# One gated pair of linear attention blocks: kv and M in head blocks of 120, 120 and 80 features a half, and M read back in two loads

## Chip, cores, metric

One core of a Trainium2 chip. The metric is the device time of one execution in microseconds, the median of the runs; lower is better. All times below are in microseconds unless ns is written.

The engines by the names of the profile: PE is TensorE (PEld its weight loads), DVE VectorE, ACT ScalarE, POOL GpSimd, SP SyncE. SP and ACT both issue DMAs, each on a queue of its own.

## The reference

Two linear attention blocks, A and B, read the same `x` (2048 rows, 640 features, 32 heads of 20), each with its own weights; a gate of each row mixes their outputs.

```python
def _A_ref(x, wqkv, wo):          # B is the same with its own weights
    B, S, D = x.shape
    H = 32; Dh = D // H
    qkv = (x @ wqkv).reshape(B, S, 3, H, Dh).transpose(2, 0, 3, 1, 4)
    q, k, v = qkv[0], qkv[1], qkv[2]
    phi = lambda t: jnp.where(t > 0, t + 1, jnp.exp(t)) + 1e-6
    pq, pk = phi(q), phi(k)
    kv = jnp.einsum("bhsd,bhse->bhde", pk, v)
    z = jnp.einsum("bhsd->bhd", pk)
    num = jnp.einsum("bhqd,bhde->bhqe", pq, kv)
    den = jnp.einsum("bhqd,bhd->bhq", pq, z)[..., None] + 1e-6
    return (num / den).transpose(0, 2, 1, 3).reshape(B, S, D) @ wo

g = sigmoid((x * gate_w).sum(-1, keepdims=True))
out = g * a + (1 - g) * b
```

## The kernel before

**What is computed instead of the reference's steps.** The kernel never forms `v`. It builds G = transpose(x) times phi(k), 640 by 640 (the two tiles `GT`, the left and the right 320 columns, the "halves"), and from it kv = transpose(wv) times G, of which only the 20 by 20 blocks of the heads on the diagonal are wanted. kv and the output weights give one 640 by 640 matrix M = kv wo for each branch. The output is then phi(q) of A, scaled by the gate and the denominators, times M of A, plus the same of B. Both large products and most of the others are done with fewer multiplications by sums and differences of quarters (the functions named `strassen`, the products `p1` to `p7` of a `Pair`).

**Order.** Everything from line 955 on is issued in the order in which it is written (`manual_schedule`). Each engine, and each DMA queue, works its own instructions in that order. The program goes: keys and queries of A (to some 50), G of A (50 to 71), keys and queries of B, with the kv of A as one fill between two of its products (72 to 114), M of A and G of B (114 to 139), kv and M of B (137 to 143), and from 141 on the output products, in eight `Pair`s of row blocks.

**kv.** `kv_mm` (L630) makes the diagonal blocks in strips. The 640 output features are cut into six blocks, `f_rows` (L99): five of 120 features, which are six heads, and a last one of 40. `e_rows` (L98) are the 120 weight columns of each, the last one taken from 520 to 640. The block from 240 to 360 lies across the two halves of G, so `pieces` (L100) has seven entries, with two for this block. Each piece is five matmuls, one for each 128 rows of the contraction: the weights of v are the stationary operand (128 rows, 120 columns), and 120, 80 or 40 columns of G are the moving one. The results stand in two PSUM banks, blocks 0 to 3 in the first. `kv_mask` (L641) multiplies them on DVE with `maskE` (L106, built on POOL at L186 to L191), which keeps the head blocks, and writes bf16 into `kv6`.

**M.** `m_block` (L652) multiplies one masked block with its 120 rows of wo: two matmuls of 320 columns. `wo_sb` (`load_wo`, L883) has wo laid out by these blocks; it comes in two DMAs. `m_a` (L667) and `m_b` (L675) copy the result out of PSUM and `m_store` (L664) writes the block's rows to a scratch in HBM, `m_rows`. From there M is read back with five consecutive rows in each partition, which is the layout that the output products need: A's in one load (L552), B's with `m_load` (L683).

**A's kv and M.** The class `Masks` (L1028) is the second fill of the first `q_strassen` of B: its matmuls are issued there, then its masks in two steps (`clamp`, `top`) between other DVE work. It also issues the load of wv of B, in four DMAs. Next in TensorE's order after kvA is the product of L417 that goes on in the bank `co`, which DVE reads at L435 just before. A's M blocks follow at L1062 to L1064 and L551.

**B's kv and M.** `kv_low` (L1068) is called by `g_strassen` (L599) between the two last products of G: the first three pieces, which need only the left half of G. Behind them stand M blocks 0 and 1 (L1075), then the PSUM pool is exchanged for the pool `outer` with six banks, z0, z1, x0, x1, w0, w1 (L1082), which stand where slots 0, 1 and 3 of the old pool were. Then come the other four pieces with their masks, M blocks 2 to 5 among the first output product (`pairs[4].p1`), and three loads of M: blocks 0 and 1 issued by ACT, 2 and 3 and then 4 and 5 by SP. While M comes back, TensorE works on the products that don't need M of B: `p1` of all eight pairs and `p5` of four. The first that needs it is `pairs[0].p2`. `m_b` copies each half block out of PSUM, the first half on ACT, the second on ACT for blocks 0 and 1 and on DVE for the others.

Of the kernel before, what the change touches and what calls it, by code (L numbers as in the profile page):

```python
# [9 lines left out]
P = 128  # L10
FP32 = mybir.dt.float32
BF16 = mybir.dt.bfloat16
ACT = mybir.ActivationFunctionType
ALU = mybir.AluOpType

S, D, H = 2048, 640, 32
Dh = D // H
DT = D // P
# [4 lines left out]
HF = D // 2  # L23
TW = 4
NG = 6
K6 = 120
# [7 lines left out]
def kernel(  # L34
# [11 lines left out]
    nc = tc.nc  # L46
# [4 lines left out]
    persist = ctx.enter_context(tc.tile_pool(name="persist", bufs=1))  # L51
    wpool = ctx.enter_context(tc.tile_pool(name="wpool", bufs=1))
# [34 lines left out]
    def ps(name, slot=None):  # L87

        return banks(ps_raw(name, slot))
# [5 lines left out]
    GT = [persist.tile([P, DT, HF], BF16, name=f"GT{n}") for n in range(2)]  # L95
    M = [persist.tile([P, DT, D], BF16, name=f"M{b}") for b in "AB"]
    wo_sb = [None, None]
    e_rows = [slice(k, k + K6) for k in list(range(0, DT * K6, K6)) + [D - K6]]  # L98
    f_rows = [slice(k, min(k + K6, D)) for k in range(0, D, K6)]  # L99
    pieces = [(g, lo, hi) for g, f in enumerate(f_rows) for lo, hi in (  # L100
        (f.start, min(f.stop, HF)), (max(f.start, HF), f.stop)) if lo < hi]
    ident = persist.tile([P, P], BF16, name="ident")
    I4 = persist.tile([P, H], BF16, name="I4")
    zE = persist.tile([P, 2 * D], BF16, name="zE")
    E4 = zE[:, D:2 * D]
    maskE = persist.tile([P, K6], BF16, name="maskE")  # L106
    spread = persist.tile([P, P], BF16, name="spread")
    R = persist.tile([P, 2, 4, RB], BF16, name="R")
    kv6 = [R[:].rearrange("p h j n -> p (h j n)"), zE[:]]
# [32 lines left out]
    wo_dram = [A_wo, B_wo]  # L142
# [41 lines left out]
        out=spread[:].rearrange("p (h t) -> p h t", t=TW), in_=I4[:, :, None].to_broadcast([P, H, TW])  # L184
    )
    nc.gpsimd.memset(maskE[:], 1.0)  # L186
    for sign, base in ((1, 0), (-1, Dh - 1)):
        nc.gpsimd.affine_select(
            out=maskE[:], in_=maskE[:], pattern=[[-sign * Dh, K6 // Dh], [0, Dh]],
            compare_op=ALU.is_ge, fill=0.0, base=base, channel_multiplier=sign,  # L190
        )  # L191
    nc.gpsimd.memset(E4, 1.0)
    for r in range(4):
        rows = slice(32 * r, 32 * r + 32)
# [432 lines left out]
        nc.vector.tensor_copy(out=zsel[:], in_=pt[:, 0, HF:HF + DT * H].rearrange("p (c h) -> p c h", h=H))  # L627
        return zsel

    def kv_mm(b, banks, pieces, cs=range(DT)):  # L630

        for g, f0, f1 in pieces:
            hf = f0 // HF
            at = f0 - (g - g % 4) * K6
            for k, c in enumerate(cs):
                nc.tensor.matmul(
                    banks[g // 4][:K6, at:at + f1 - f0], lhsT=wv[b][:, c, e_rows[g]],
                    rhs=GT[hf][:, c, f0 - hf * HF:f1 - hf * HF], start=(k == 0), stop=(k == DT - 1),
                )

    def kv_mask(b, banks, g0, g1):  # L641

        n = f_rows[g0].stop - f_rows[g0].start
        count, lo = g1 - g0, f_rows[g0].start
        at = lo - (g0 - g0 % 4) * K6
        nc.vector.tensor_tensor(
            out=kv6[b][:K6, lo:lo + count * n].rearrange("p (g n) -> p g n", g=count),
            in0=banks[g0 // 4][:K6, at:at + count * n].rearrange("p (g n) -> p g n", g=count),
            in1=maskE[:K6, None, K6 - n:K6].to_broadcast([K6, count, n]), op=ALU.mult,
        )  # L650

    def m_block(b, g, banks, to=None):  # L652

        at = f_rows[g].start
        for hf in range(2):
            nc.tensor.matmul(
                banks[hf][:K6, 0:HF], lhsT=kv6[b][:K6, at:at + K6], rhs=wo_sb[b][:K6, g, hf * HF:(hf + 1) * HF],
                start=True, stop=True,
            )
        if to is None:  # L660
            to = work.tile([P, D], BF16, tag="osb", name="m5", bufs=3)
        return to[:f_rows[g].stop - at]

    def m_store(g, to):  # L664
        nc.sync.dma_start(out=m_rows[f_rows[g], :], in_=to)

    def m_a(g, slot):  # L667

# [6 lines left out]
    def m_b(g, banks):  # L675

        to = m_block(1, g, banks, held["mb"][:, g, :] if g < DT else None)
        n = to.shape[0]
        for hf, copy in enumerate((nc.scalar.copy, nc.scalar.copy if g < 2 else nc.vector.tensor_copy)):
            copy(out=to[:, hf * HF:(hf + 1) * HF], in_=banks[hf][:n, 0:HF])  # L680
        m_store(g, to)

    def m_load(g0, g1, eng):  # L683

        rows = slice(f_rows[g0].start, f_rows[g1 - 1].stop)
        eng.dma_start(
            out=M[1][rows.start // DT:rows.stop // DT], in_=m_rows[rows, :].rearrange("(p m) d -> p m d", m=DT)
        )

    def cells(pt):  # L690
        return [pt[:, hf] for hf in range(2)]
# [184 lines left out]
    def load_w(b, which, eng, cuts=(0, DT)):  # L876
        lo = {"q": 0, "k": D, "v": 2 * D}[which]
        t = wpool.tile([P, DT, D], BF16, tag="w" + which, name=f"w{which}{'AB'[b]}")
        for c0, c1 in zip(cuts, cuts[1:]):
            eng.dma_start(out=t[:, c0:c1], in_=wq_dram[b][:, c0:c1, lo:lo + D])  # L880
        return t

    def load_wo(b, eng):  # L883
        wo_sb[b] = wpool.tile([P, NG, D], BF16, tag="wo", name=f"wo{'AB'[b]}")
        eng.dma_start(out=wo_sb[b][:K6, 0:DT], in_=wo_dram[b][0:DT * K6].rearrange("(j p) f -> p j f", p=K6))
        eng.dma_start(out=wo_sb[b][:K6, DT], in_=wo_dram[b][e_rows[DT], :])

    class Nothing:

# [65 lines left out]
    with tc.manual_schedule():  # L955
# [72 lines left out]
        class Masks:  # L1028

            def __init__(self, slot):  # L1030
                self.pt = ps("kvA", slot)
                kv_mm(0, cells(self.pt), pieces)
                wv[1] = load_w(1, "v", nc.sync, (0, 1, 2, 3, DT))

            def clamp(self):
                kv_mask(0, cells(self.pt), 0, 4)

            def top(self):
                kv_mask(0, cells(self.pt), 4, 5)
                kv_mask(0, cells(self.pt), 5, 6)  # L1040

        f = fifth(0, quad[1:3])
# [23 lines left out]
        held["mb"] = wpool.tile([P, DT, D], BF16, tag="wk", name="MBr")  # L1066

        def kv_low():  # L1068
            held["kv"] = cells(ps("kvB", 2))
            kv_mm(1, held["kv"], pieces[:3])  # L1070
            kv_mask(1, held["kv"], 0, 2)

        g_strassen(1, 1, 0, 3, kv_low)
        kv = held["kv"]
        for g, slot in enumerate((3, 0)):  # L1075
            m_b(g, cells(ps("mB", slot)))
        new_stage(None)
        outer = ctx.enter_context(late_pool("outer"))
        t = wpool.tile([P, 2, DT, HF], BF16, tag="wq", name="TM12")
# [1 line left out]
        half = ST // 2  # L1081
        acc = {k: [bank(outer, f"o{k}{n}") for n in range(2)] for k in "zxw"}  # L1082
        pairs = [Pair(i) for i in range(half)]
        kv[1] = acc["x"][1]
        kv_mm(1, kv, pieces[3:5], (2, 3, 4, 0, 1))
        kv_mask(1, kv, 2, 4)
        kv_mm(1, kv, pieces[5:], (2, 3, 4, 0, 1))
        for g in (4, 5):
            kv_mask(1, kv, g, g + 1)
        spare = cells(ps("mB", 2))  # L1090
        pairs[4].p1(None, (0, 1))
        m_b(2, acc["w"])
        m_b(3, spare)
        pairs[4].p1(None, (2, 3, 4))
        m_b(4, acc["z"])
        m_b(5, acc["w"])
        m_load(0, 2, nc.scalar)
        pairs[4].p1_out()
        for g in (2, 4):
            m_load(g, g + 2, nc.sync)  # L1100
        scale(1, 4)
        for rows, ks in ((0, (1,)), (1, (1,)), (0, (2, 4))):
            p_sums(part[rows], ks)
        for k, to in ((5, None), (6, spare[0]), (7, acc["z"][0]), (2, acc["w"][0]), (3, acc["w"][1])):
            pairs[k].p1(to)
        held["p5"] = wpool.tile([P, 2, HF], FP32, tag="wv", name="p5s")
        pairs[0].p1()
# [73 lines left out]
```

## Time and profile before

| | us |
|---|---|
| median of 3 runs (185.88 to 185.99) | 185.98 |
| the profiled execution | 185.64 |
| its span, first to last instruction | 183.90 |
| DVE busy | 149.0 (81%) |
| ACT busy | 108.4 (59%) |
| POOL busy, all of it in the first 10.5 | 9.1 (5%) |
| kv of B on TensorE, 25 + 10 matmuls | 137.6 to 141.3 |
| stores of M of B, first and last issue | 140.74, 144.03 |
| loads of M of B: ACT, SP, SP issue | 143.53, 145.27, 148.28 |

The granted clock of TensorE is 1.0 throughout. The span is what the instructions of the profile cover; the rest of the execution's time lies around it. A line of a timeline or of the chain begins with its start in the span and its length. A line of a group gives what is written from what, shape, count, then busy time and the mean duration in ns of one, then the engine's idle time before them. Matmuls are pipelined, so that the durations of neighbours overlap; what one costs TensorE is the time from its start to the next one's.

### The profile page before, as it was taken

What the parts mean: (1) busy time and instruction counts of PE and PEld (TensorE: products, weight loads), DVE (VectorE), ACT (ScalarE), POOL (GpSimd) and SP (SyncE); (2) the same over time, 40 slices, a digit from 0 to 9 for tenths busy, and PEclk for the clock granted to TensorE, in tenths of its full rate; (3) what the DMA queues carried; (4) which work ended last, traced back from release to release, by engine and by line L of the source; (5) the groups of instructions that cost most, each with busy time, mean ns of one, the idle gap of its engine ahead of it and who ended that gap; (6) DMA issues with size and microseconds to landing.
All of it is one profiled execution on the core that took longest, in us unless ns stands there. A gap on an engine that the chain in (4) does not pass through costs nothing.

```text
span 183.9 us, 3530 instructions
## 1 busy us (share of the span) xinstructions
PE 179.7 (98%) x1357; PEld 121.0 (66%) x1357; DVE 149.0 (81%) x263; ACT 108.4 (59%) x207; POOL 9.1 (5%) x25
## 2 busy tenths in 40 slices
PE   8999999999999999999999999999999999999993
PEld 3656657665667667676666655777678767777772
DVE  0488988999899799798898987969795978778854
ACT  2155589976883553776778787873814637453210
POOL 8920000000000000000000000000000000000000
PEclk9999999999999999999999999999999999999999
DMA  6995449985018000004100000144901820322232
GB/s 182 323 141 86 100 100 302 344 166 179 0 40 249 11 4 0 0 0 133 50 0 0 4 0 2 35 133 144 239 13 42 232 84 4 123 91 77 71 126 88
DMA packets 20896, 18.01 MB, mean 98 GB/s; under 512 B 9168, under 2 KB 20624, under 8 KB 20880
## 3 DMA queue, kind: packets, MB, share of 16 engines
q1 hardware_dynamic: 19952, 16.67, 33.0%
q10 hardware_dynamic: 928, 1.13, 1.9%
q8 instruction: 10, 0.16, 0.4%
q14 instruction: 6, 0.05, 0.1%
HBM read 11.54 MB, written 4.28 MB: 86 GB/s over the span
## 4 chain that ended last, share of the span: by engine, by line
PE 91%; DMA 4%; DVE 2%; ACT 1%; issue 0%; SPq 0%; DVEq 0%
PE gs L519 17%; PE kB L299 12%; PE q L417 11%; PE kA L299 11%; PE qA L352 7%; PE oy L774 6%; PE oz L774 4%; PE ox L774 3%; PE ow L774 3%; PE q L352 3%; PE gA L489 2%; PE gB L489 2%; DMA m_rows<-m 2%; PE warm L211 2%; DMA MB<-m_rows 1%; PE qB L352 1%
## 5 line engine op out<-in xcount | busy, mean ns | idle before, releaser
L299 PEld LDWEIGHTS <-xT 128*128 128x128 bf16 x320 | 30.9, 98 | 14.9 <-DVE xT L257 0.2
L276 DVE TENSOR_SCALAR e<-e 128x640 bf16<-128x640 bf16 (+2 forms) x58 | 20.0, 346 | 6.0 <-ACT e L268 5.6
L299 PE MATMUL kB<-wkB,xT 128*128 128x320 bf16 x160 | 24.2, 299 | 0.0
L299 PE MATMUL kA<-wkA,xT 128*128 128x320 bf16 (+1 forms) x160 | 23.2, 299 | 0.0
L268 ACT ACTIVATE e<-q 128x512 bf16<-128x512 f32 x26 | 15.7, 603 | 5.3 <-PE q L417 4.3
L268 ACT ACTIVATE e<-kB 128x640 bf16<-128x640 f32 x16 | 11.4, 710 | 7.6 <-PE kB L299 7.5
L519 PEld LDWEIGHTS <-xn 128*128 128x128 bf16 x128 | 12.3, 98 | 5.4 <-issue 0.6
L268 ACT ACTIVATE e<-kA 128x640 bf16<-128x640 f32 x16 | 11.3, 713 | 7.4 <-PE kA L299 7.3
L352 PE MATMUL qA<-xT,wqA 128*128 128x512 bf16 x60 | 13.4, 379 | 0.1
L352 PEld LDWEIGHTS <-wqA 128*128 128x128 bf16 x64 | 7.5, 117 | 6.1 <-issue 0.3
L837 ACT COPY u<-ox 128x320 f32<-128x320 f32 x8 | 3.4, 426 | 12.4 <-PE ox L774 12.4
L287 DVE SCALAR_TENSOR_TENSOR pk<-kB,e 128x640 bf16<-128x640 f32 x12 | 9.9, 823 | 1.0
L774 PEld LDWEIGHTS <-pqTB 128*128 128x128 bf16 x80 | 7.7, 98 | 3.7 <-issue 0.7
L774 PEld LDWEIGHTS <-xT 128*128 128x128 bf16 x85 | 8.1, 98 | 2.9
L774 PEld LDWEIGHTS <-pqTA 128*128 128x128 bf16 x85 | 8.0, 98 | 2.9
L779 DVE TENSOR_TENSOR osb<-oz,u 128x320 bf16<-128x320 f32 (+1 forms) x18 | 8.0, 453 | 2.3 <-PE oz L774 1.8
L519 PE MATMUL gs<-pk,xn 128*128 128x320 bf16 x64 | 9.4, 299 | 0.0
L287 DVE SCALAR_TENSOR_TENSOR pk<-kA,e 128x640 bf16<-128x640 f32 x10 | 8.2, 822 | 0.9 <-DVE e L276 0.2
L435 DVE TENSOR_TENSOR q<-q,p 128x512 f32<-128x512 f32 x12 | 8.3, 693 | 0.8 <-PE q L417 0.6
L268 ACT ACTIVATE e<-qA 128x1024 bf16<-128x1024 f32 x6 | 6.2, 1028 | 4.4 <-PE qA L352 4.2
L489 PEld LDWEIGHTS <-xn 128*128 128x128 bf16 x64 | 6.2, 98 | 3.2 <-issue 0.3
L519 PEld LDWEIGHTS <-S 128*128 128x128 bf16 x64 | 6.0, 98 | 2.6 <-issue 0.5
(193 smaller groups left out, 358.5 us busy)
## 6 DMA issues: line engine op xcount, KB each, us to landing
out_dram<-osb SPq DMA_DIRECT2D x14, 160.0 KB, 1.8
xn<-in_A_x_dram SPq DMA_DIRECT2D x3, 640.0 KB, 6.3
wvA<-in_A_wqkv_dram SPq DMA_DIRECT2D x1, 800.0 KB, 10.1
wkB<-in_B_wqkv_dram SPq DMA_DIRECT2D x1, 800.0 KB
wqB<-in_B_wqkv_dram SPq DMA_DIRECT2D x1, 800.0 KB, 6.5
MA<-m_rows SPq DMA_DIRECT2D x1, 800.0 KB, 4.6
woA<-in_A_wo_dram SPq DMA_DIRECT2D x1, 750.0 KB, 12.5
m_rows<-MA SPq DMA_DIRECT2D x5, 150.0 KB, 2.0
```

Of the source, the lines that this page charges most:

```text
L211: nc.tensor.matmul(warm[:, 0, 0:n], lhsT=one_l, rhs=one_r[:, 0:n], start=True, stop=True)
L268: nc.scalar.activation(out=to, in_=part, func=ACT.Exp)
L276: nc.vector.tensor_scalar(self.e, self.e, 1.0, EPS, op0=ALU.min, op1=ALU.add)
L287: nc.vector.scalar_tensor_tensor(out=dst, in0=src, scalar=1.0 + EPS, in1=e, op0=ALU.add, op1=ALU.max)
L299: nc.tensor.matmul(pt[:, hf, 0:n], lhsT=xT[:, c, i * P:(i + 1) * P], rhs=wk[b][:, c, hf * HF:hf * HF + n], start=(c == 0), stop=(c == DT - 1),
L352: nc.tensor.matmul(dst, lhsT=mixed(wq[b][:, c, :], m), rhs=xT[:, c, n * HB:(n + 1) * HB], start=first, stop=last,)
L417: nc.tensor.matmul(dst, lhsT=left(c), rhs=right(c), start=first and k == 0, stop=k == len(cs) - 1, skip_group_check=not first,)
L435: nc.vector.tensor_tensor(out=dst, in0=src, in1=sb, op=ALU.add)
L489: nc.tensor.matmul(pt[:, hf, 0:HF], lhsT=xn[:, i, c * P:(c + 1) * P], rhs=pk[:, i, hf * HF:(hf + 1) * HF], start=(i == 0), stop=(i == ST - 1),
L519: nc.tensor.matmul(pt[:, n, 0:HF], lhsT=left[:, i, n * P:(n + 1) * P], rhs=right[:, i, :], start=(first and i == 0), stop=(i == hc - 1), s ...
L774: nc.tensor.matmul(dst, lhsT=left[:, c, r0:r0 + P], rhs=right[:, c, :], start=(first and c == 0), stop=(c == DT - 1), skip_group_check=not ...
L779: nc.vector.tensor_tensor(out=dst, in0=acc, in1=sb, op=ALU.add)
```

## The change

The cuts follow the halves. Each half of 320 features has blocks of 120, 120 and 80 features (`blocks`), so that none lies across the middle; kv has six pieces for seven, and every block has as many rows of weights as it has features. The first half's kv stands in the first PSUM bank, the second's in the second. `maskE` becomes 320 wide, made of three parts with two selects each. `wo_sb` is laid out by half and block and comes in three DMAs for two; wv of B comes in three for four. A's masks are four pieces for three.

For B, the low three blocks are masked in `kv_low`, and their M blocks 0 to 2 stand together ahead of the second half's kv, in banks of the new pool and in slot 2. The three high blocks are masked one by one, and their M blocks 3 to 5 are issued among the five matmuls of `pairs[4].p1`, which now stands in bank w0. Blocks 0, 3 and 4 have their second half copied by DVE, the others by ACT. The last block has 80 rows for 40. M is read back in two loads of 320 rows, both issued by SP behind all six stores.

```diff
-    e_rows = [slice(k, k + K6) for k in list(range(0, DT * K6, K6)) + [D - K6]]
-    f_rows = [slice(k, min(k + K6, D)) for k in range(0, D, K6)]
-    pieces = [(g, lo, hi) for g, f in enumerate(f_rows) for lo, hi in (
-        (f.start, min(f.stop, HF)), (max(f.start, HF), f.stop)) if lo < hi]
+    blocks = [slice(hf * HF + lo, hf * HF + hi) for hf in range(2) for lo, hi in ((0, K6), (K6, 2 * K6), (2 * K6, HF))]
...
-    maskE = persist.tile([P, K6], BF16, name="maskE")
+    maskE = persist.tile([P, HF], BF16, name="maskE")
...
-    for sign, base in ((1, 0), (-1, Dh - 1)):
-        nc.gpsimd.affine_select(
-            out=maskE[:], in_=maskE[:], pattern=[[-sign * Dh, K6 // Dh], [0, Dh]],
-            compare_op=ALU.is_ge, fill=0.0, base=base, channel_multiplier=sign,
-        )
+    for lo in range(0, HF, K6):
+        part = maskE[:, lo:min(lo + K6, HF)]
+        for sign, base in ((1, 0), (-1, Dh - 1)):
+            nc.gpsimd.affine_select(
+                out=part, in_=part, pattern=[[-sign * Dh, part.shape[1] // Dh], [0, Dh]],
+                compare_op=ALU.is_ge, fill=0.0, base=base, channel_multiplier=sign,
+            )
...
-    def kv_mm(b, banks, pieces, cs=range(DT)):
+    def rows_in(g):
+        return blocks[g].stop - blocks[g].start
+
+    def kv_mm(b, banks, gs, cs=range(DT)):
 
-        for g, f0, f1 in pieces:
-            hf = f0 // HF
-            at = f0 - (g - g % 4) * K6
+        for g in gs:
+            hf, n = g // 3, rows_in(g)
+            part = slice(blocks[g].start - hf * HF, blocks[g].stop - hf * HF)
             for k, c in enumerate(cs):
                 nc.tensor.matmul(
-                    banks[g // 4][:K6, at:at + f1 - f0], lhsT=wv[b][:, c, e_rows[g]],
-                    rhs=GT[hf][:, c, f0 - hf * HF:f1 - hf * HF], start=(k == 0), stop=(k == DT - 1),
+                    banks[hf][:n, part], lhsT=wv[b][:, c, blocks[g]], rhs=GT[hf][:, c, part],
+                    start=(k == 0), stop=(k == DT - 1),
                 )
...
     def kv_mask(b, banks, g0, g1):
...
+        n, hf = rows_in(g0), g0 // 3
+        at = slice(blocks[g0].start, blocks[g1 - 1].stop)
+        part = slice(at.start - hf * HF, at.stop - hf * HF)
+        nc.vector.tensor_tensor(out=kv6[b][:n, at], in0=banks[hf][:n, part], in1=maskE[:n, part], op=ALU.mult)
...
-                banks[hf][:K6, 0:HF], lhsT=kv6[b][:K6, at:at + K6], rhs=wo_sb[b][:K6, g, hf * HF:(hf + 1) * HF],
+                banks[hf][:n, 0:HF], lhsT=kv6[b][:n, blocks[g]], rhs=wo_sb[b][:n, g // 3, g % 3, hf * HF:(hf + 1) * HF],
...
-        nc.sync.dma_start(out=m_rows[f_rows[g], :], in_=to)
+        nc.sync.dma_start(out=m_rows[blocks[g], :], in_=to)
...
-        for hf, copy in enumerate((nc.scalar.copy, nc.scalar.copy if g < 2 else nc.vector.tensor_copy)):
+        for hf, copy in enumerate((nc.scalar.copy, nc.scalar.copy if g in (1, 2, 5) else nc.vector.tensor_copy)):
...
-        eng.dma_start(out=wo_sb[b][:K6, 0:DT], in_=wo_dram[b][0:DT * K6].rearrange("(j p) f -> p j f", p=K6))
-        eng.dma_start(out=wo_sb[b][:K6, DT], in_=wo_dram[b][e_rows[DT], :])
+        wo_sb[b] = wpool.tile([P, 2, 3, D], BF16, tag="wo", name=f"wo{'AB'[b]}")
+        halves = wo_dram[b].rearrange("(h r) f -> h r f", h=2)
+        for h in range(2):
+            eng.dma_start(
+                out=wo_sb[b][:K6, h, 0:2], in_=halves[h, 0:2 * K6].rearrange("(j p) f -> p j f", p=K6)
+            )
+        eng.dma_start(out=wo_sb[b][:HF - 2 * K6, :, 2], in_=halves[:, 2 * K6:HF].rearrange("h p f -> p h f"))
...
-                kv_mm(0, cells(self.pt), pieces)
-                wv[1] = load_w(1, "v", nc.sync, (0, 1, 2, 3, DT))
+                kv_mm(0, cells(self.pt), range(6))
+                wv[1] = load_w(1, "v", nc.sync, (0, 1, 3, DT))
 
             def clamp(self):
-                kv_mask(0, cells(self.pt), 0, 4)
+                kv_mask(0, cells(self.pt), 0, 2)
+                kv_mask(0, cells(self.pt), 2, 3)
 
             def top(self):
-                kv_mask(0, cells(self.pt), 4, 5)
+                kv_mask(0, cells(self.pt), 3, 5)
                 kv_mask(0, cells(self.pt), 5, 6)
...
         def kv_low():
-            held["kv"] = cells(ps("kvB", 2))
-            kv_mm(1, held["kv"], pieces[:3])
-            kv_mask(1, held["kv"], 0, 2)
+            kv = cells(ps("kvB", 2))
+            kv_mm(1, kv, range(3))
+            kv_mask(1, kv, 0, 2)
+            kv_mask(1, kv, 2, 3)
 
         g_strassen(1, 1, 0, 3, kv_low)
-        kv = held["kv"]
-        for g, slot in enumerate((3, 0)):
-            m_b(g, cells(ps("mB", slot)))
         new_stage(None)
...
-        kv[1] = acc["x"][1]
-        kv_mm(1, kv, pieces[3:5], (2, 3, 4, 0, 1))
-        kv_mask(1, kv, 2, 4)
-        kv_mm(1, kv, pieces[5:], (2, 3, 4, 0, 1))
-        for g in (4, 5):
-            kv_mask(1, kv, g, g + 1)
+        for g, k in enumerate("wz"):
+            m_b(g, acc[k])
         spare = cells(ps("mB", 2))
-        pairs[4].p1(None, (0, 1))
-        m_b(2, acc["w"])
-        m_b(3, spare)
-        pairs[4].p1(None, (2, 3, 4))
+        m_b(2, spare)
+        for g in range(3, 6):
+            kv_mm(1, [None, acc["x"][g > 3]], [g], (2, 3, 4, 0, 1))
+        for g in range(3, 6):
+            kv_mask(1, [None, acc["x"][g > 3]], g, g + 1)
+        pairs[4].p1(acc["w"][0], (0, 1))
+        m_b(3, [acc["w"][1], acc["x"][0]])
+        pairs[4].p1(acc["w"][0], (2,))
         m_b(4, acc["z"])
-        m_b(5, acc["w"])
-        m_load(0, 2, nc.scalar)
+        m_b(5, spare)
+        pairs[4].p1(acc["w"][0], (3, 4))
         pairs[4].p1_out()
-        for g in (2, 4):
-            m_load(g, g + 2, nc.sync)
+        m_load(0, 3, nc.sync)
+        m_load(3, 6, nc.sync)
...
-        for k, to in ((5, None), (6, spare[0]), (7, acc["z"][0]), (2, acc["w"][0]), (3, acc["w"][1])):
+        for k, to in ((5, None), (6, acc["x"][0]), (7, acc["w"][1]), (2, acc["z"][0]), (3, acc["z"][1])):
             pairs[k].p1(to)
```

## Prediction

> **What bounds the kernel now.** I read busy time first, then who waits for whom on TensorE, then the chain that ended last, then the timeline at each place that the change touches.
>
> ```profile
> PE 179.7 (98%) x1357; PEld 121.0 (66%) x1357; DVE 149.0 (81%) x263; ACT 108.4 (59%) x207; POOL 9.1 (5%) x25
> ```
>
> TensorE is busy 98% of the span, so time is gained by fewer or cheaper matmuls, or from its few waits. Its own waits are two:
>
> ```profile
> PE warm L211 <- PEq L1165: 0.8, 1, 0.8
> PE ow L774 <- DMA MB<-m_rows: 0.4, 1, 0.4
> ```
>
> The first is the start. The second is M of B, read back late. The chain shows why, and the timeline what it costs:
>
> ```profile
> 139.65 0.55 PE mB L656 x4
> 140.20 0.55 PE kvB L636 x10
> 140.75 0.52 PE ox L636 x10
> ...
> 144.03 4.16 DMA m_rows<-m
> ...
> 148.28 2.54 DMA MB<-m_rows
> 150.82 0.14 issue
> ```
>
> ```profile
> 149.81 0.71 PE L774 MATMUL oz<-TM,pqTA 128*128 128x320 bf16 x4
> 150.95 0.30 PE L774 MATMUL ow<-MB,pqTB 128*128 128x320 bf16 x1 [0.44 <-DMA MB<-m_rows]
> ```
>
> Matmuls of 320 columns overlap: five take 0.68 in the chain, 0.136 each from start to start, though each lasts 0.30. The last filler ends at 150.52, so started at 150.22; the next could have started at 150.36 and did at 150.95. The wait costs 0.59, not 0.44.
>
> **Fewer kv matmuls.** Before, each kv has 7 pieces of 5 matmuls, since the block at 240 to 360 is cut at the middle; afterwards 6 blocks, 4 of 120 and 2 of 80. What one costs:
>
> ```profile
> 80.81 1.89 PE kvA L636 x35
> ```
>
> ```profile
> L636 PEld LDWEIGHTS <-wvA 128*120 128x120 bf16 x35 | 2.1, 135 | 0.2
> L218 PEld LDWEIGHTS <-zsel 128*32 128x32 bf16 x80 | 2.0, 96 | 0.6 <-issue 0.5
> ```
>
> 1.89 over 35 is 0.054. The ten at 140.20 hold five of 40 columns and five of 120 and take 0.055 each, so the width of the moving operand doesn't matter: the load of 120 weight columns does. Five matmuls fewer give at least 5 x 0.055 = 0.27 for each kv. No row has 80 weight columns. Its load lies between 96 ns at 32 and 135 at 120, by a line 117, which is 18 ns less, so 0.037 a matmul; L621 and L622 at 124.61 to 124.98, 10 in 0.37, show that 0.037 can be had. Upper end 0.055, no gain. I take 0.037, as the loads set the pace: 20 x 0.055 + 10 x 0.037 = 1.47 against 1.92, 0.45 for each kv (0.27 at the other end).
>
> For kvA something else is next:
>
> ```profile
> 81.46 0.69 DVE L435 TENSOR_TENSOR q<-q,p 128x512 f32<-128x512 f32 x1
> 82.55 0.38 PE L417 MATMUL q<-SQ,MB 128*128 128x512 bf16 x1
> ```
>
> The matmul behind kvA adds into the bank that this VectorE sum reads until 82.15. With the 0.05 that TensorE needs after a VectorE release (11.23 to 11.28 further down) it can't start before 82.20, so kvA gives at most 0.35. **kvA: 0.35; kvB: 0.45**, as the sum that gates kvB's last columns (L597) follows TensorE's own matmuls.
>
> **The three low M blocks early.** Before, two M blocks stand ahead of the second part of kv and four behind it; now three and three. The same 12 matmuls of 0.136, so nothing on TensorE. What moves is the stores. From 139.49, less 0.09 for kv_low's 80-wide piece, I lay the new order out with the old pitches: blocks 0 to 2 end at 140.2, kv at 140.96, block 3 starts at 141.23, block 4 at 141.64, block 5 at 141.91 (before: 142.61). ScalarE now has nine copies and VectorE three (before eight and four) at about 0.33 and 0.49; ScalarE's last ends near 143.05. The last store goes at **143.1** instead of 144.03, and no block waits for its operand: masks 3, 4 and 5 are done at 140.98, 141.23 and 141.38.
>
> **Two loads on SP.** The old last store took 4.16 where the median of its line is 2.1: ScalarE's queue had issued a 300 KB load of M at 143.53, ahead of it. Now all loads stand behind all stores on SP's queue, so I take 2.1 to 2.4 for the last one, down at 145.4 (upper end 4.16). The first load waits for stores 0 to 2 (the third issues at 141.64, down at 143.75). The second waits for the last store and issues at 145.4. Its size, 400 KB, has no row:
>
> ```profile
> 149.00:149.50 0.50, 0.50 (x6) 0.39 (x4) 0.50 (x1) 0.25 (x1) 0.00 (x0) 1.00 0.94 205
> 149.50:150.00 0.50, 0.50 (x6) 0.35 (x4) 0.28 (x1) 0.16 (x1) 0.00 (x0) 1.00 0.54 205
> ```
>
> The old last load alone, 200 KB, moves for 1.0 of its 2.54. At that rate 400 KB take 3.5; between 200 KB (2.54) and the 800 KB of MA (4.6) 3.2; the 300 KB load among others took 4.0. I take 3.5, plus 0.4 for waiting behind the first load's tail: M is down at 149.3. TensorE wants it at 150.36 - 0.45 = 149.9, less 0.13 for the release. Margin 0.5, so **the whole 0.59 goes**. Late next would be TM on VectorE (0.99), which pair 0 needs ten matmuls, 1.36, after its start: 150.4 against 151.3, no wait. The Trainium skill (SBUF — State Buffer, "Door 1: The DMA port swizzle") says that partitions 0 to 63 reach no more of SBUF's DMA ports than 0 to 31, so that a 64-partition load is no faster per byte than a 32-partition one; by this rule the load takes the same 3.5, and the 205 GB/s of the old 32-partition load agrees with its 189 to 196.
>
> **Costed at nothing.** A's masks: a 480, a 120 and a 40 column piece (0.65, 0.27, 0.19) become two of 240 (0.41) and two of 80 (about 0.23): 0.17 more on VectorE, which idles 0.39 before 85.92. B's masks, 0.15 more: the first 80 piece falls into the 0.68 idle before 139.69. SP's extra wo DMAs (0.4 to 0.5 each, up to 2.5 at A's, where issuing itself is held up): behind A's, SP waits until 41.8 for wkB; behind B's, until 140.7. wvB is one DMA less. A's last store has 80 rows for 40; TM waits 0.2 for MA, and VectorE then idles 0.90 before 132.31. No ScalarE DMA: 0.4 off an engine that doesn't bound.
>
> maskE takes 6 selects for 2 and a longer memset, some 1.3 more on POOL (0.32 each for 120 columns). POOL is idle later, but not here:
>
> ```profile
> 9.36 0.72 POOL L196 TENSOR_SCALAR_AFFINE_SELECT zE<-zE 32x640 bf16<-32x640 bf16 x1
> 9.52 0.73 DVE L276 TENSOR_SCALAR e<-e 128x640 bf16<-128x640 bf16 x1 [1.56 <-ACT e L268]
> ...
> 10.41 0.82 DVE L287 SCALAR_TENSOR_TENSOR pk<-kA,e 128x640 bf16<-128x640 f32 x1 [0.15 <-DVE e L276]
> ...
> 11.28 0.59 PE L352 MATMUL qA<-xT,wqA 128*128 128x512 bf16 x2
> ```
>
> The same VectorE form takes 0.32 elsewhere; here 0.73, until just after POOL's select. TensorE's qA needs the bank that L287 reads: its last matmul before starts at 10.91, and 0.14 later it could go on; it does at 11.28, 0.23 lost. Which POOL instruction runs at 9.52 afterwards I can't read. Not held up, 0.23 is gained; held up for a whole 0.72 select, 0.17 is lost. I take 0. The Trainium skill (SBUF — State Buffer, "Who interferes with whom") has GpSimd and a VectorE tensor_scalar of this sort lock one shared port pair, the later blocking fully; the 0.73 agrees, and by it more POOL work can only move this loss.
>
> **Sum**: 0.59 + 0.35 + 0.45 = 1.39 off the span of 183.9, whose execution took 185.64. The median of the runs is 185.98, 0.34 above that one; I subtract from the median: **184.6**.
>
> **Rivals.** (1) 80-wide loads cost the same as 120: 0.59 + 0.27 + 0.27 = 1.13, 184.85. For: nothing has been seen between 32 and 120. (2) Readback stays on the path a little: the last store takes 3.1 (halfway to 4.16) and the load 4.0, M down at 143.1 + 3.1 + 0.1 + 4.0 = 150.3, TensorE resumes at 150.43 instead of 150.95; 0.52 + 0.35 = 0.87 gained, 185.1. For: a margin of only 0.5. (3) POOL holds VectorE up by the whole select: 184.6 + 0.17 = 184.8. For: the row at 9.52. The Trainium skill's lock, named above, would do just this. (4) A new wait: block 0 now writes a bank of the pool that follows, and if that waits until the old pool's last reader (L597, ends 140.18 - 0.09) is done, TensorE stands from 139.41 to 140.14: 184.6 + 0.73 = 185.3. Against: the reader is of another bank. (5) Slower: the two 400 KB loads are the worse cut. If store rows are again served behind a load (4.16, down at 147.26) and the last load is as slow as MA's (4.6), M is down at 151.95, TensorE resumes at 152.08, 1.13 later than before, less kvA's 0.35: 186.8. It loses from a landing after 151.17. Against: that load is behind the store on one queue. (6) The change doesn't bring what it says: the time on kv comes back as waits on VectorE at 38 to 115, and M's wait stays: 186.0. Against: VectorE and ScalarE idle for TensorE there (7.5 on ScalarE for kB).
>
> **Chances.** Forecast 0.42, (1) 0.13, (2) 0.14, (3) 0.08, (4) 0.07, (5) 0.09, (6) 0.07. Time 184.6. The range goes from the forecast with POOL's 0.23 gained, 184.37, and 0.1 of rounding, to (4) and a little of (2): 184.2 to 185.5; (5) and (6), 0.16, are left out. What can be told from no change is 0.2%, 0.37: faster 0.84 (the forecast and 1 to 4), same 0.07 (6), slower 0.09 (5).
>
> **What will show it.** Kv groups of 30 matmuls: kvA in about 1.5 with the next matmul some 0.35 after the old one's place; 80-column loads near 117 ns (135 says rival 1). The last m_rows store landing within 2.4 of its issue, and no TensorE wait on MB; a wait left there says (2) or (5). The VectorE row near 9.5 at 0.32 or 0.73 tells (3). A gap ahead of the first mB matmul says (4). The prediction is wrong if TensorE's waits turn up in a place that I have called covered.

## The result, and the profile after

The changed kernel takes **184.88** (184.13 to 185.62, 12 runs) where the kernel before takes 185.93 beside it (185.55 to 186.49, 12 runs): a ratio of 0.9938, 95% interval 0.9919 to 0.9956. A second series, beside later experiments, gave 184.91 against 186.33, 0.9923 (0.9909 to 0.9937). So it is 1.05 to 1.42 faster; the forecast was 184.6, in a range of 184.2 to 185.5. The profiled execution took 185.31, with a span of 183.6 (before: 185.64 and 183.9).

The busy times of the changed kernel's page, then TensorE's waits:

```profile
PE 179.2 (98%) x1337; PEld 120.4 (66%) x1347; DVE 148.2 (81%) x264; ACT 108.6 (59%) x208; POOL 10.3 (6%) x29
```

```profile
PE warm L210 <- PEq L1166: 0.8, 1, 0.8
PE ow L772 <- DMA MB<-m_rows: 0.2, 1, 0.2
```

TensorE has ten weight loads fewer (1347 for 1357), five for each kv, as the cut says; its matmul records are 20 fewer, so ten are missing from the trace of after. The wait on M of B has not gone. It is smaller: 0.24 of idle time where it was 0.44. The chain of waits and TensorE's timeline show it at its place:

```profile
143.49 1.88 DMA m_rows<-m
...
145.51 4.98 DMA MB<-m_rows
150.49 0.14 issue
```

```profile
149.27 1.11 PE L772 MATMUL oz<-TM,pqTA 128*128 128x320 bf16 x7
150.63 1.11 PE L772 MATMUL ow<-MB,pqTB 128*128 128x320 bf16 x7 [0.24 <-DMA MB<-m_rows]
```

Seven matmuls at 0.136 from 149.27 are the end of the work that needs no M of B, so the next could have started at 150.22. It starts at 150.63, 0.41 late (0.60 before, by the same reckoning). The last store landed even a little sooner than the forecast's 2.1 to 2.4: 1.88 for the old 4.16. The load behind it did not keep to the forecast: 4.98 for 3.9.

kvA came as forecast. Here are its matmuls, VectorE's sum, and the matmul that waits for it; the first row is from the kernel before:

```profile
80.65 2.05 PE L636 MATMUL kvA<-GT,wvA 128*120 128x120 bf16 x35
```

```profile
81.25 1.66 PE L638 MATMUL kvA<-GT,wvA 128*120 128x120 bf16 x30
...
82.06 0.69 DVE L434 TENSOR_TENSOR q<-q,p 128x512 f32<-128x512 f32 x1
...
82.81 0.38 PE L416 MATMUL q<-SQ,MB 128*128 128x512 bf16 x1
```

From kvA's first matmul to the next product it is 82.81 - 81.25 = 1.56 (82.55 - 80.65 = 1.90 before): 0.34 less. The sum ends at 82.75, and the product starts 0.06 later. The weight loads of both widths, in the view of line 638 (shortest, median and longest, in ns):

```profile
L638 PEld LDWEIGHTS <-wvA x30: 117/135/140, 81.0 to 82.7; 128*120 128x120 bf16 x20, 128*80 128x80 bf16 x10
```

The 80-column loads take 117 to 123 ns, and their matmuls follow each other at 35 to 39 ns, those of 120 at 55. All that comes later is counted from the start of kvB's first matmul, before and after:

```profile
137.60 0.97 PE L636 MATMUL kvB<-GT,wvB 128*120 128x120 bf16 x15
```

```profile
137.86 0.90 PE L638 MATMUL kvB<-GT,wvB 128*120 128x120 bf16 x15
```

### The profile page after: what moved, and what is told of

It is laid out like the page before. It is cut to its first block, busy times and chain, and to the rows that moved or that the text cites. A ratio compares the mean times of both kernels' runs of the same rounds, so it can differ in the third digit from the quotient of the medians.

```text
span 183.6 us, 3504 instructions
## 1 busy us (share of the span) xinstructions
PE 179.2 (98%) x1337; PEld 120.4 (66%) x1347; DVE 148.2 (81%) x264; ACT 108.6 (59%) x208; POOL 10.3 (6%) x29
## 4 chain that ended last, share of the span: by engine, by line
PE 93%; DMA 4%; DVE 1%; issue 0%; SPq 0%; ACT 0%
PE gs L518 17%; PE kA L298 12%; PE kB L298 12%; PE q L416 11%; PE qA L351 7%; PE oy L772 6%; PE oz L772 4%; PE ow L772 3%; PE ox L772 3%; DMA MB<-m_rows 3%; PE q L351 2%; PE gA L488 2%; PE gB L488 2%; PE warm L210 2%; PE qB L351 1%; DMA m_rows<-m 1%
## 5 line engine op out<-in xcount | busy, mean ns | idle before, releaser
L298 PE MATMUL kA<-wkA,xT 128*128 128x320 bf16 (+1 forms) x160 | 24.0, 306 | 0.1
```

What stands on the lines that cost most here:

```text
L298: nc.tensor.matmul(pt[:, hf, 0:n], lhsT=xT[:, c, i * P:(i + 1) * P], rhs=wk[b][:, c, hf * HF:hf * HF + n], start=(c == 0), stop=(c == DT - 1),
```

## The experiments

Each of the timed ones has five rounds beside the kernel before. Numbers without another word are from the profiled execution. "kvB" is the start of kvB's first matmul, "M down" the end of the last load of M of B in the chain, "lost at M" what TensorE loses by starts at the first product that needs M of B.

**One load of M instead of two.**

```diff
-        m_load(0, 3, nc.sync)
-        m_load(3, 6, nc.sync)
+        m_load(0, 6, nc.sync)
```

> M of B is read back in one load of 640 rows (128 partitions, 800 KB) behind all six stores, instead of two loads of 320 rows. Theory (the half loads are slow because each fills only 64 partitions: 205 GB/s in 147.0 to 148.0 of the changed kernel's profile, 348 to 435 for the 128-partition load of MA): issue near 145.5 after the shift of that run, landing 4.4 later as MA's, TensorE's wait on MB gone or under 0.1, so 0.3 to 0.4 less than the changed kernel; against the kernel before -1.5, ratio 0.992. Rival (what counts is the bytes that are still to come when the last store lands): 800 KB behind the last store instead of 400, landing near 5.5 to 6 after issue, TensorE waits 0.9 to 1.4, that is 0.5 to 1.0 more than the changed kernel; ratio 0.997 to 0.999.

184.88 (ratio 0.9926, 0.9903 to 0.995). In this execution TensorE lost 0.02 at M of B (149.33 + 6 x 0.136 = 150.15):

```profile
149.33 0.98 PE L772 MATMUL oz<-TM,pqTA 128*128 128x320 bf16 x6
150.16 1.53 PE L772 MATMUL ow<-MB,pqTB 128*128 128x320 bf16 x10
```

That looked like the proof that two loads of 64 partitions are the worse form. The repeat below takes it back.

**Three loads, all on SP.**

```diff
-        m_load(0, 3, nc.sync)
-        m_load(3, 6, nc.sync)
+        for g in (0, 2, 4):
+            m_load(g, g + 2, nc.sync)
```

> M of B is read back in three loads on SP (240, 200 and 200 rows; 48, 40 and 40 partitions), all behind the six stores. Theory (64-partition halves one behind the other): the first two loads go out 0.5 and 0.2 earlier, the last is 256 KB; last landing near 3.6 to 4.0 after an issue at 145.5, so 149.1 to 149.5, no wait on MB, 0.4 less than the changed kernel, ratio 0.992. Rival (a fixed cost for each load, so that two are better than three): last landing at 150.5 or later, nothing gained or 0.2 lost against the changed kernel, ratio 0.994 to 0.995.

185.05 (0.9938, 0.9915 to 0.9961); 0.63 lost at M. The last load, of 200 rows only, took 5.38 behind the two others, so that M was down at 150.42. The landing that I expected was missed by about 1, and the rival's 150.5 is nearer.

**The cut alone**, with the old order, the old shares of the copies and the three loads of before:

```diff
-        for g, k in enumerate("wz"):
-            m_b(g, acc[k])
+        for g, slot in enumerate((3, 0)):
+            m_b(g, cells(ps("mB", slot)))
...
-        m_load(0, 3, nc.sync)
-        m_load(3, 6, nc.sync)
+        m_load(0, 2, nc.scalar)
+        pairs[4].p1_out()
+        for g in (2, 4):
+            m_load(g, g + 2, nc.sync)
```

> The new blocks, masks and wo layout, but the order of before: M blocks 0 and 1 ahead, four behind, copies as before, and three loads (240 rows on ACT, 200 and 200 on SP). Theory (the cut gives 0.34 at kvA and 0.39 at kvB, the order of stores and loads gives the part of the wait): those two stay, and the wait on MB grows, as TensorE comes 0.39 earlier and the last store has 80 rows and stands behind the load on ACT's queue again (4 us to landing): 0.8 to 1.1 lost there, net 0.5 to 0.8 below the kernel before, ratio 0.996 to 0.997. Rival (order and loads bring nothing): same as the changed kernel, ratio 0.994, wait on MB as the 0.41 there.

185.98, ratio 0.9999 (0.9982 to 1.0016): nothing. kvA still gives its 0.35, and the wait on M takes 1.33 where it took 0.60. The chain shows the store behind a load again:

```profile
143.49 4.27 DMA m_rows<-m
...
147.82 3.21 DMA MB<-m_rows
```

**The old, narrow mask in the changed kernel** (two selects on POOL for the mask in place of six, and one mask broadcast over the blocks):

```diff
-    maskE = persist.tile([P, HF], BF16, name="maskE")
+    maskE = persist.tile([P, K6], BF16, name="maskE")
...
+            in1=maskE[:n, None, 0:n].to_broadcast([n, count, n]), op=ALU.mult,
```

> The changed kernel with the mask of 120 columns of before (two selects on POOL instead of six, broadcast when it is read), so that POOL's list is that of before and ends near 10.4 instead of 11.6. Theory (POOL's selects hold the first clamp of VectorE, L275, up when it arrives in one): where the clamp arrives in a select it takes up to 0.73 instead of 0.32 and TensorE's step from kA to qA takes up to 0.38 instead of 0.14; which of the two happens depends on when TensorE's clock comes up in that execution. Against the changed kernel 0 to 0.24 slower in the median, ratio to before 0.994 to 0.996. Rival (the masks' broadcast read, not POOL, matters): the clamp takes 0.32 always and only the masks' rows change.

184.65 (0.9929, 0.9904 to 0.9954), not to be told from the changed kernel. VectorE's first clamp (the `TENSOR_SCALAR` on `e`, 0.32 to 0.33 when nothing holds it up) took 0.78 here, and 0.33 in the changed kernel with three times the selects for the mask (first POOL's select and the clamp in this run, then the clamp in the changed kernel):

```profile
9.37 0.72 POOL L193 TENSOR_SCALAR_AFFINE_SELECT zE<-zE 32x640 bf16<-32x640 bf16 x1
```

```profile
9.49 0.78 DVE L273 TENSOR_SCALAR e<-e 128x640 bf16<-128x640 bf16 x1 [1.56 <-ACT e L265]
```

```profile
10.36 0.33 DVE L275 TENSOR_SCALAR e<-e 128x640 bf16<-128x640 bf16 x1 [1.56 <-ACT e L267]
```

In the second execution of the changed kernel it arrives at 9.58 and takes 0.33, but the clamp after it, at 10.80, takes 0.65. So the amount of POOL's work does not decide it; the moment of arrival does. In seven of the fourteen traces (before, this run, and the runs with three loads, the cut with one load, no wait, one load again, and one load with the narrow mask) the first clamp arrives 0.27 or more before the end of one of POOL's selects, and each time it ends 0.18 to 0.19 after that select, whether it arrived early in it (and took 0.78, here) or late (0.46). In the other seven it arrives in the last 0.11 of a select, and takes 0.33.

**The readback alone**: the kernel before with one load behind all stores.

```diff
-        m_load(0, 2, nc.scalar)
         pairs[4].p1_out()
-        for g in (2, 4):
-            m_load(g, g + 2, nc.sync)
+        m_load(0, NG, nc.sync)
```

> The kernel before, with its three loads of M (300 KB on ScalarE's queue, two of 200 KB on SP's) replaced by one load of 640 rows on SP's queue behind all six stores; nothing else of the change. My theory: the wait on M of B came from the way of the readback alone, not from the order of the M blocks or the cut. The last store, issued near 144.0, is no longer served behind a load and lands in 1.9 to 2.1 instead of 4.16; the one load takes 3.9 to 4.1, so M is down near 150.1 and TensorE's wait of 0.59 shrinks to 0.0 to 0.1: 0.5 to 0.6 less, 185.4 to 185.5. Rival: without the early third block the load starts too late, M is down after 150.4 and half or more of the wait stays: 185.7 or more.

185.99 against 186.13, ratio 0.9986 (0.9972 to 1.0). The rival came true: 0.47 is lost at M, for 0.60 before. The last store lands sooner (the load starts 2.34 after its issue), but the load of 800 KB takes 4.41, and M is down 6.75 after the last store's issue where it was 6.79.

**The cut, the old order and the old shares of the copies, one load.**

> The kernel with the new cut, the old order of blocks 2 to 5 and of their copies, and one load of 640 rows on SP's queue behind the stores. My theory: with one load the order of the M blocks is worth nothing that can be measured: the last store is issued at 143.4 to 143.6 as in both kernels with the new cut, lands 1.9 to 2.1 later, the load takes 3.9 to 4.1, M is down at 149.2 to 149.7 where TensorE wants it near 149.9: no wait, 184.7 to 185.1 as with one load in the new order. Rival: the three early blocks are needed too; then a wait of 0.3 or more on M of B is left and the time is 185.2 or more.

185.76, ratio 0.9976 (0.9963 to 0.999). The rival came true again: 0.72 is lost at M.

```profile
143.97 1.83 DMA m_rows<-m
...
146.50 4.48 DMA MB<-m_rows
```

The last store is issued 6.38 behind kvB, in the changed kernel 5.63. And the work that needs no M of B ends hardly sooner than before. Two rows of the timeline say where the time of the cut goes; the third is from the kernel before:

```profile
139.62 0.49 DVE L596 TENSOR_TENSOR GT<-gs,u 128x320 bf16<-128x320 f32 x1 [0.54 <-PE gs L518]
...
140.16 0.90 PE L638 MATMUL ox<-GT,wvB 128*120 128x120 bf16 x15
```

```profile
140.03 0.71 PE L636 MATMUL kvB<-GT,wvB 128*120 128x40 bf16 x10
```

With two M blocks ahead of it, kv of the right half would start at 139.96, but it starts at 140.16, just after VectorE's sum ends at 140.11; 0.20 is lost. The sum does write an operand of this kv, but one that only the fifth matmul reads, at 140.18 from a start at 139.96. What the first matmul waits for is its bank: `x1` of the new pool stands where the sum's input stands, and in the program that the kernel builds (its list of instructions with their semaphore waits) this matmul has the wait for the sum. In the kernel before, the first ten matmuls of the right half wrote kvB's own bank, and they started at 140.03 while the sum ran until 140.18. 0.16 more goes at 141.3 to 141.6, at M block 3, whose weight load waits 0.27 for its mask. In the new order block 2's two matmuls, 0.27 long, lie in the first hole, and the second isn't there.

**A lone load of 64 partitions**: the first half is loaded early, so only the second goes behind the stores.

```diff
+        m_load(0, 3, nc.sync)
         for g, k in enumerate("wz"):
...
-        m_load(0, 3, nc.sync)
         m_load(3, 6, nc.sync)
```

> The changed kernel with its first load of M (rows 0 to 319) moved ahead of all stores, so that it reads rows of M of A (the output of B's first half of M is left wrong in this way: that half is A's); the second load, 64 partitions and 400 KB, then goes alone behind the stores. It measures what a lone 64-partition load takes. My theory: 64 partitions move at the rate of 32 (205 GB/s), so it takes 2.0 of moving and 1.5 to 1.9 around it, 3.5 to 3.9 where it took 4.98 behind the other half: the prediction's 3.5 was right for a lone load and its 0.4 for the tail of the first was short by about 1. Rival: the load takes 4.5 or more alone too; then the 3.5 was wrong by itself.

189.82, in a single execution: the stores overwrite the rows that the early load reads, so SP issues them only from 144.13 on. What was to be measured can still be read, in the chain and in the windows (the last number is GB/s):

```profile
149.33 4.20 DMA MB<-m_rows
```

```profile
150.00:150.50 0.50, 0.41 (x4) 0.07 (x1) 0.00 (x0) 0.00 (x0) 0.00 (x0) 1.00 0.00 0
150.50:151.00 0.50, 0.00 (x0) 0.00 (x0) 0.00 (x0) 0.00 (x0) 0.00 (x0) 1.00 0.96 154
151.00:151.50 0.50, 0.00 (x0) 0.00 (x0) 0.00 (x0) 0.00 (x0) 0.00 (x0) 1.00 0.63 243
151.50:152.00 0.50, 0.00 (x0) 0.00 (x0) 0.00 (x0) 0.00 (x0) 0.00 (x0) 1.00 1.34 371
152.00:152.50 0.50, 0.00 (x0) 0.00 (x0) 0.00 (x0) 0.00 (x0) 0.00 (x0) 1.00 0.26 51
```

4.20, between what the two theories gave. The four windows hold 0.5 x (154 + 243 + 371 + 51) = 410 KB, moved in about 2.0; the other 2.2 are 1.2 ahead of the first bytes and 1.0 behind the last.

**No wait on the readback at all**: one load ahead of all stores.

```diff
+        m_load(0, 6, nc.sync)
         for g, k in enumerate("wz"):
...
-        m_load(0, 3, nc.sync)
-        m_load(3, 6, nc.sync)
```

> The changed kernel with one load of M of B ahead of all stores, so that it reads M of A and nothing waits for the stores (B's output is made with A's M). It bounds what any way of the readback can give. My theory: with one load behind the stores nothing of the readback is left on the path, so this is the same as that kernel: 184.7 to 185.0, and no wait on M of B. Rival: the readback still costs through the queues (its transfers delay the loads of x or TM's operands): 184.5 or less.

B's output is then made with M of A. 184.77 (0.9925, 0.9904 to 0.9946); nothing is lost at M. The time is no other than with the wait of 0.2 to 0.4, within an interval of 0.4 either way. What is left in the readback is less than these runs can tell.

**The changed kernel once more, one load once more, one load with the narrow mask**, on one chip:

> The changed kernel itself, once more, to stand on the same chip beside the next two. My theory: its wait on M of B is there in every execution (0.3 to 0.5 in the profile), so it is 0.2 to 0.4 above the kernel with one load: 184.9 to 185.2. Rival: what the wait costs is given back behind it; then the two are the same within 0.1.

> The changed kernel with one load of 640 rows for its two of 320, once more beside the changed kernel. My theory: no wait on M of B, 0.2 to 0.4 less than the changed kernel of this same series. Rival: the same within 0.1.

> One load of 640 rows and the 120-wide mask of the kernel before (two selects on POOL for six), the two edits together. My theory: the width of the mask is worth nothing that can be measured (whether the clamp is held up goes by when it arrives among POOL's selects), so this is within 0.15 of the kernel with one load alone. Rival: fewer selects on POOL hold VectorE up less often; then it is 0.2 to 0.3 below.

184.91, 185.03 and 184.91; ratios 0.9923, 0.993 and 0.9929. The rival of the first two holds: 0.12 apart, with intervals of 0.3 either way, they can't be told apart. In this execution the kernel with one load lost 0.42 at M and the changed one 0.23, the other way round than in the first pair (0.02 and 0.41). TensorE's rows of the repeat with one load, then of the changed kernel's repeat:

```profile
149.21 0.98 PE L772 MATMUL oz<-TM,pqTA 128*128 128x320 bf16 x6
150.45 1.26 PE L772 MATMUL ow<-MB,pqTB 128*128 128x320 bf16 x8 [0.26 <-DMA MB<-m_rows]
```

```profile
149.30 0.30 PE L772 MATMUL oz<-TM,pqTA 128*128 128x320 bf16 x1
149.67 1.52 PE L772 MATMUL ow<-MB,pqTB 128*128 128x320 bf16 x10
```

So the form of the load is worth nothing that these runs can tell, and neither is the width of the mask; no version is clearly faster than the changed kernel.

**The new order with the old shares of the copies.** It splits the order on TensorE from the shares of the copies.

```diff
-        for hf, copy in enumerate((nc.scalar.copy, nc.scalar.copy if g in (1, 2, 5) else nc.vector.tensor_copy)):
+        for hf, copy in enumerate((nc.scalar.copy, nc.scalar.copy if g < 2 else nc.vector.tensor_copy)):
```

> The changed kernel with the old shares of the copies: ScalarE copies both halves of blocks 0 and 1, VectorE the second half of blocks 2 to 5 (so VectorE has four, with block 2's and block 5's for block 0's). It splits the earlier last store of the changed kernel, 5.63 behind kvB's first matmul against 6.43 before, into the order of the blocks on TensorE and the shares of the copies. My theory: the order alone brings most of it. Block 5's second half then waits on VectorE behind block 4's copy until near 142.9 less 0 and takes 0.4: last store at 5.5 to 5.8, the kernel within 0.2 of the changed one. Rival: block 2's copy on VectorE pushes the masks of blocks 3 to 5 back by its 0.49, TensorE's blocks 3 to 5 with them, and the last store is at 6.1 or later: 0.3 or more slower than the changed kernel.

**186.28** against 186.01, ratio 1.0009 (0.9995 to 1.0023): without this one line the whole gain is gone. The rival was right, and by more than it said. TensorE's waits, then the timeline, then two rows of the changed kernel for comparison:

```profile
PE ow L654 <- DVE zE L648: 0.8, 1, 0.8
PE ow L772 <- DMA MB<-m_rows: 0.3, 1, 0.3
```

```profile
141.25 0.44 ACT L678 CAST MBr<-mB 80x320 bf16<-80x320 f32 x1
141.72 0.49 DVE L678 CAST MBr<-mB 80x320 bf16<-80x320 f32 x1 [1.39 <-ACT MBr L678]
142.13 0.60 DVE L648 TENSOR_TENSOR zE<-ox,maskE 120x120 bf16<-120x120 f32 x3
142.45 0.35 PE L654 MATMUL ow<-woB,zE 120*120 120x320 bf16 x1 [0.82 <-DVE zE L648]
```

```profile
140.98 0.28 DVE L648 TENSOR_TENSOR zE<-ox,maskE 120x120 bf16<-120x120 f32 x1 [0.21 <-PE ox L638]
...
141.52 0.30 PE L654 MATMUL ow<-woB,zE 120*120 120x320 bf16 x1
```

Block 2's second half stands on VectorE's queue ahead of the masks of blocks 3 to 5. It starts when ScalarE is done with the first half, and ScalarE comes to that only at 141.25, behind four copies of blocks 0 and 1. This wait is in the program: the two halves of blocks 2 and 5 are one PSUM tile (`spare`), and in the list of instructions VectorE's copy of the second half waits for the count that ScalarE's copy of the first raises. Where the halves are two tiles it waits for TensorE alone, and the copies overlap (block 3: 142.84 and 142.97, 0.42 and 0.49 long). In the new shares ScalarE copies both halves of both these blocks. With the old ones the masks start at 142.13 for 140.98, TensorE loses 0.99 at block 3, and the last store goes 6.86 behind kvB.

Not tried are the new shares in the old order, and the new order and shares with the old cut. So the runs show that the gain needs the new shares, and not how much the shares bring without the rest.

## Why the prediction was right, point by point

In this table a kernel's first two numbers, added, less the third and with 0.05 to 0.14 for the release, give what TensorE loses. ("M wanted" is the start that TensorE would have had without the wait. The ratios are each to the kernel before of the same series.)

| kernel | last store's issue behind kvB | from there to M down | M wanted behind kvB | lost at M | ratio |
|---|---|---|---|---|---|
| before | 6.43 | 6.79 | 12.75 | 0.60 | 1 |
| readback alone | 6.42 | 6.75 | 12.75 | 0.47 | 0.9986 |
| cut alone | 6.38 | 7.54 | 12.72 | 1.33 | 0.9999 |
| cut, one load | 6.38 | 7.01 | 12.72 | 0.72 | 0.9976 |
| changed | 5.63 | 7.00 | 12.36 | 0.41 | 0.9938 |
| changed, one load | 5.63 | at most 6.70 | 12.36 | 0.02 | 0.9926 |
| changed, one load, again | 5.64 | 7.10 | 12.37 | 0.42 | 0.993 |
| changed, three loads | 5.64 | 7.22 | 12.37 | 0.63 | 0.9938 |
| changed, old copies | 6.86 | 6.90 | 13.39 | 0.50 | 1.0009 |

"M wanted" and the loss together say when the products with M of B start. By them, and with 0.34 for kvA where the cut is in, the readback alone should gain 0.13 (the runs gave 0.14), the cut with one load 0.25 (0.37), the changed kernel 0.92 (1.05 and 1.42), without any wait 1.33 (1.36), and with the old copies 0.20 should be lost (0.27). The cut alone is off: 0.36 lost by the trace, 0.0 by the runs.

- **kvA, 0.35**: 0.34, with its cap. VectorE's sum decides, not the number of matmuls.
- **80-column loads, 117 ns and 0.037 a matmul**: measured 117 to 123 ns and 0.035 to 0.039. Rival 1, at 135 ns, falls. The step from the one to the other was partly luck: the length of a load does not set the pace by itself, for the rows of L621 and L622 that the prediction took as its example have loads of 128 columns, 0.12 to 0.13 long, and go at 0.037 all the same.
- **kvB, 0.45**: 0.39 arrived (12.75 - 12.36). But it hangs on the order: with the cut and the old order it is 0.03 (12.72), for the bank that VectorE's sum reads and VectorE's masks hold the rest. The prediction added it as if it came with the cut.
- **No block waits for its operand, and the last store goes at 143.1**: it went 5.63 behind kvB where the forecast had 143.1 - 137.60 = 5.50. Right, with the new shares of the copies; with the old ones TensorE stands for 0.99. The prediction counted both engines' copies and did not see how much hangs on VectorE's share.
- **The last store, 2.1 to 2.4**: 1.88. **The load behind it, 3.5 + 0.4**: 4.98. This is the term that was mis-sized. A lone load of 64 partitions takes 4.20, so 0.7 was missing there, and standing behind the first half costs 0.8 for 0.4. The prediction took 1.54 around the moving from the load of 200 KB; it is 2.2. So from the last store's issue to M there are 7.0 for the forecast 6.2, and of the 0.59 only 0.19 went (0.37 in the second execution). The parts of the 0.19: the store goes 0.80 earlier, less 0.21 of longer readback, less 0.39 since TensorE comes sooner: 0.20.
- **The way of the readback** was given the credit for that wait. The table says otherwise: by three loads, two or one it is 6.7 to 7.2 from the last store to M, but for the cut alone (7.54). What one gains on the store behind no load, one gives back on the larger load.
- **POOL, 0**: no difference showed. In the profile of before the clamp cost 0.24, in that of after nothing; but with the list of selects of before it was not held up in the kernel with the readback alone (0.33 at 10.04), and with the new list it was in three other kernels (0.71 to 0.76). It goes by the moment of arrival, so rival 3 falls as a mechanism of this change.
- **Rival 2**, the readback that stays on the path a little, is what the trace shows; the measured 184.88 lies between its 185.1 and the forecast 184.6. Rivals 4, 5 and 6 did not come: no gap ahead of the first M block, no store behind a load. But what rival 4 feared for block 0, a bank of the new pool that waits for the old pool's last reader, is what costs kv of the right half 0.20 with the old order. The cut alone, 185.98, has the time of rival 6 by another way (its 0.34 at kvA stays, and the wait on M takes it back), and with the old copies, 186.28, the gain is lost by a mechanism that none of the rivals named.

The sum by the trace is 0.34 + 0.39 + 0.19 = 0.92 (1.10 with the second execution's wait), and the runs gave 1.05 and 1.42, for 1.39 forecast. That the second series meets the forecast does not confirm its 0.59: in the two executions a third and two thirds of that wait went, and the two series differ by 0.37 themselves. The two spans differ by 0.3 only: 0.92, and 0.24 for the clamp, less 0.83 that TensorE's start cost in this one execution of after, which the last section shows.

## What to carry to other kernels

The parts of such a change don't add: the cut alone gave 0.0, the readback in one load alone 0.1, the cut with it 0.4, and everything but the new shares of the copies nothing (1.0009, with 1 in the interval), while all together gave 1.05 to 1.42. When work is moved forward on one engine, look first at what stands ahead of its operand on the other engine's queue, and at who still reads the bank that it writes. And a wait of a few tenths behind a round trip through HBM scatters by as much from one execution to the next (0.02 and 0.42 for the same kernel), so that one trace of each does not rank two forms of it.

## What the runs showed of the hardware

TensorE's start varies between executions of one kernel. The first rows of kA in the changed kernel, first execution and second:

```profile
5.02 2.08 PE L298 MATMUL kA<-wkA,xT 128*128 128x320 bf16 x8
```

```profile
4.82 1.37 PE L298 MATMUL kA<-wkA,xT 128*128 128x320 bf16 x8
```

The eight take 0.7 longer in the first (most of them 0.267 from start to start, for 0.136), and everything behind them stands that much later, though the granted clock is listed as 1.0 for both executions. The listed share leaves out what comes ahead of the first entry of the trace's clock record. That entry is the change to full clock, at 6.71 in this execution, where the slow matmuls end, and at 5.05 in the kernel before. The 1.66 between the two, run at half the pace, make the 0.83 by which the third group of kA stands later (8.04 for 7.21). The Trainium skill (TensorE: Matmul & The Clock Gate, "Part 1: The HAM clock gate (the "warmup" mystery)") tells of a free-running window, so that the number of slow matmuls at the start varies from run to run; these two rows agree.

A load of 400 KB over 64 partitions takes 4.20 alone, one of 800 KB over 128 takes 4.2 to 4.56 in the five executions that have it behind the stores. The Trainium skill (SBUF — State Buffer, "Door 1: The DMA port swizzle") has partitions 0 to 63 reach half of the ports; the mean of the lone load, 410 KB in about 2.0, 205 GB/s, agrees, beside the 410 GB/s that the load over 128 partitions reaches in its best half microsecond in the kernel with the readback alone. The single windows do not all agree: one of the four above reads 371 (a packet counts whole in the window where it starts). So what makes the half load as slow as the whole one is not shown here.

VectorE's clamp and POOL's selects hold each other up: a clamp that arrives 0.27 or more before the end of a select ends 0.18 to 0.19 after it (seven traces), and a select that starts while a clamp runs takes up to 0.83 for 0.72 (the cut alone, where the clamp runs from 9.62 to 9.95 and the select from 9.69 to 10.52).
